# A top-32 attention feeding an MLP on one Trainium2 core: loads and stores on two DMA queues, weight preparation shared with GpSimd, new planner constants

## The chip, the cores and the metric

The kernel runs on one core of a Trainium2 chip. The metric is the device time of one execution in microseconds (us). Before the change it is 886.87 us, the median of three runs (886.37 to 887.69).

The engines are called here as the profile calls them: PE is TensorE (matmuls; PEld its weight loads), DVE is VectorE, ACT is ScalarE, POOL is GpSimd, SP is SyncE, which issues DMAs. Each engine works through its own list of instructions strictly in order.

## The reference

```python
# q, k, v: (4 batches, 8 heads, 576, 64) float32
scores = q @ k.T / sqrt(64)
kth    = 32nd largest of each row
attn   = softmax(where(scores >= kth, scores, -1e9))
x      = (attn @ v), heads side by side        # (2304, 512)
h      = x @ w_in                              # w_in (512, 2048)
g      = h * tanh(softplus(h))
return g @ w_out                               # w_out (2048, 512)
```

The two weight matrices arrive as 64-bit floats; everything else is float32.

## The kernel before, in words

The kernel holds three kinds of work, which one planner interleaves.

**Attention.** The unit of work (`unit`) is a tile of 128 query rows of a pair of heads; it has two "slots", one for each head (a last half tile of 64 rows has one slot), 144 slots in all. For a slot PE makes the scores (L604), ACT evicts them to SBUF as S (L621), DVE takes the eight largest of each of eight chunks of 72 columns (L636, eight per slot) and from these the first 24 of the row (L646, L650). Then all scores above the 24th are counted and masked, either by ACT with a Sign (L665) or by DVE (L669), POOL multiplies the mask with S (L673), a small instruction on DVE writes nine sentinels behind the row (L676), and DVE finds the 32nd largest from the rest (L679). ACT takes the exponential (L722) and DVE masks and sums it (L724). PE transposes the result (L769), ACT evicts it, PE multiplies with V (L805). K of a pair of heads is loaded by five DMAs (`dk`, L493 to L498), V by three (`dvl`, L526 to L530), a tile of Q by one (L571), all on SP.

**The weights.** `piece` takes 32 blocks of 128 x 512 numbers, 16 of `w_in` and 16 of `w_out`. Each block comes by one DMA of 512 KB on SP (L403), as pairs of 32-bit words. It is put together from the two words: a shift of the low word by 29 bits on DVE (L409), the high word scaled by ACT into PSUM (L414), and both joined by DVE (L424). The sign is taken in one of two ways: where `share(SGN, i)` is true, by a Sign on ACT (L418) and a product on POOL (L429); otherwise by one more DVE instruction (L420). All but the first six blocks of `w_out` are then split in two for the matmul's reduced format: ACT casts the high part (L440), and the low part is made either by PE and ACT (L446, L447, L450, where `share(PLO, i)` is true) or by a subtraction on POOL (L453).

**The MLP.** Nine groups of 256 tokens, each of 16 column blocks: PE multiplies with `w_in` (L906), ACT and POOL make the activation, PE multiplies with `w_out` (L975, L979). `flush` evicts a group's output (L998) and stores it (L1019, all on SP; the last group has eight stores).

**The order.** Nothing is ordered by hand. Every step is handed to `Plan.op` with an engine, an assumed duration, its dependencies, the buffers that it takes and frees, and a priority; `Plan.schedule` plays them through a model of the chip and writes the instructions out in the order that this gives. A step may name other engines in `also` (the helper `either` names POOL first, then DVE and sometimes ACT); the planner takes the one with the earliest assumed end, to which it adds an amount from `BIAS` for any but the first. The constants `MLP0`, `MLPS`, `LAG`, `OFF` and `WPO` set the priorities: of MLP groups against attention, of kinds of steps within a unit, and of `w_out` blocks. `PLO` and `SGN` are shares. For an SP step `cols` is the time that issuing takes and the duration that of the transfer:

```python
if o.eng == "sp":
    avail["sp"] = s + o.cols
    moved = max(s + o.cols + 0.65, moved) + o.dur
    o.end = moved + 0.9
```

After the plan, `rows_missed` checks on the chip that the first pass was exact, and a branch (L1071) skips a slow second pass.

Of the kernel before, what the change touches and what calls it, by code (L numbers as in the profile page):

```python
# [10 lines left out]
F32R = mybir.dt.float32r  # L11
I32 = mybir.dt.int32
AF = mybir.ActivationFunctionType
ALU = mybir.AluOpType
# [5 lines left out]
KHI = float(2.0 ** 27)  # L20
TOPK = 32
NCH = 8
PAD = 9
# [8 lines left out]
XR = 512  # L32
MLP0 = 59.16014052214167
MLPS = 1.1073074438698398
LAG = (-25.995810819941177, -17.66529125005204, -14.559786015886564, -11.242347655389478, -8.814713112832253, -7.76696476612947, -3.1712703340899724, -0.9827647919513685, -5.242546123881124)
OFF = (-9.344957211177771, 2.0041542064057873, -0.6528013842420144, 1.3086536928118269, 0.41279236860293267, 1.0938802916676011, -1.5617639856277443, 2.6926860599010802, -28.16820150226302, -2.1162741319410996, 2.930197754188401, -1.6831534370444627, 9.183328578610238)
WPO = 4.861214464413224
CSH = [(19, 0.8667247802625605), (999, 0.3323003066774938)]
MSH = [(11, 0.9149166775649588), (999, 0.13298644690001551)]
WPR = (19.149617763081373, 0.047652472774268644)  # L40
DELTA = 0
ALSO = True
N2 = 6
LOCK = True
TAB = 1.4
BIAS = [(54.23725795086648, 10.898476612244764), (712.3479862116446, 0.9005748864757063), (1000000000.0, 0.7950689159040172)]
PLO = [(11, 1.0), (999, 0.21870871979825823)]
SGN = 0.5127532531018606
PH = {3: ([0, 1], [2], [3, 4])}

SLACK = {'pe': 0.2487527268649277, 'dve': 0.0, 'act': 0.0, 'pool': 0.3}
TICK = 3.413
# [3 lines left out]
class Held(float):  # L58
    pass


# [13 lines left out]
class Plan:  # L75
# [22 lines left out]
    def schedule(self):  # L98
# [34 lines left out]
        while ndone < len(self.ops):  # L133
# [52 lines left out]
            if o.eng == "sp":  # L186
                avail["sp"] = s + o.cols
                moved = max(s + o.cols + 0.65, moved) + o.dur
                o.end = moved + 0.9
            else:  # L190
                o.end = avail[o.eng] = s + dur
                if o.eng == "pool" or isinstance(o.dur, Held):
                    port[o.eng] = o.end
# [23 lines left out]
def acts(n, bias=0, acc=0):  # L217
    return act(n, bias, acc) + 0.04
# [10 lines left out]
def dve2(n):  # L229
    return Held((0.5208 * n + 72) / 1000)  # L230
# [6 lines left out]
def pool1(n):  # L237
    return (1.03 * n + 110) / 1000
# [7 lines left out]
def attn_moe_kernel(  # L246
# [98 lines left out]
    def build(fast, weights):  # L345
# [22 lines left out]
        def share(part, n):  # L368
# [3 lines left out]
            return int((n + 1) * part) > int(n * part)  # L372

        xw = [[None] * (NT // 64) for _ in range(KC)]
        xread = [[[] for _ in range(NT // 64)] for _ in range(KC)]
# [4 lines left out]
        if weights:  # L380
# [7 lines left out]
            def piece(i, src, hi, lo, a, ready, pool):  # L388
# [12 lines left out]
                if wide:  # L401
                    val = lambda t=F32, e=0: word(e, t).rearrange("p (a b) -> p a b", a=a)
                    d = P.op("sp", 1.46, lambda: nc.sync.dma_start(  # L403
                        out=stage().bitcast(I32).rearrange("p (a b) -> p a b", a=a), in_=src),
# [75 lines left out]
            release("STG", [("HB", x) for x in range(Z["HB"] - 6, Z["HB"] - 2)])  # L480


        def pair_keys(b, p, ts, pr):
# [7 lines left out]
            def dk():  # L491
                kn_, rest = g_("KN", kn_key), k[b, 2 * p:2 * p + 2, T * 128:S, :].rearrange("h p d -> p h d")
                nc.sync.dma_start(out=kn_[:, 0:T, 1, :], in_=kap(1))  # L493
                nc.sync.dma_start(out=kn_[64:128, 0:T, 0, :], in_=kap(0)[0:64])
                nc.sync.dma_start(out=kn_[0:64, 1:T + 1, 0, :], in_=kap(0)[64:128])
                edge = kn_[0:64].rearrange("p t h d -> p (t h d)")
                for h, c_ in ((0, 0), (1, T * 2 * D + D)):
                    nc.sync.dma_start(out=edge[:, c_:c_ + D], in_=rest[:, h, :])  # L498

            kn_key = key + ("n",)  # L500
            d1 = [P.op("sp", 1.63, dk, alloc=[("KN", kn_key)], prio=pr - 3 + OFF[0], cols=2.9)]
# [23 lines left out]
            def dvl():  # L525
                nc.sync.dma_start(out=g_("V", key + ("v",)),  # L526
                                  in_=v[b, 2 * p:2 * p + 2, 0:T * 128, :].rearrange("h (p t) d -> p h t d", t=T))
                for h in range(2):
                    hp = slice(64 - 64 * h, 128 - 64 * h)
                    nc.sync.dma_start(out=vl[P.slot[key + ("v",)]][hp, h, :], in_=v[b, 2 * p + h, T * 128:S, :])  # L530

            dv = [P.op("sp", 0.9, dvl, alloc=[("V", key + ("v",))], prio=pr + OFF[2], cols=1.78)]
            return key, [v1, v2], dv

        slot_no = [0]
        shared = {}
        ends = dict(ot=[], rz=[], on=[])

        def either(tp, td, fn, deps, ta=None, fa=None, **kw):

            also = [("dve", td, lambda: fn(nc.vector))]
            if ta:
                also.append(("act", ta, fa))
            return P.op("pool", tp, lambda: fn(nc.gpsimd), deps, also=also if ALSO else (), **kw)

        def unit(b, p, t, pkey, kready, vready, last, pr, final):
# [25 lines left out]

            dq = [P.op("sp", 0.36, dql, alloc=[("QN", qn)], prio=pr - 3 + OFF[0], cols=0.5)]
            wq = key + ("wq",)
# [52 lines left out]
            if fast:  # L627
# [29 lines left out]
                for n in range(nt):  # L657
# [10 lines left out]
                    else:  # L668
# [193 lines left out]
        def group(g):  # L862
# [28 lines left out]
            for q_ in range(NQ):  # L891
                hk, hbk = ("h", g, q_), ("hb", g, q_)
                for e in range(2):
# [3 lines left out]
                    def m1(f=f, hk=hk, e=e):  # L897
# [10 lines left out]
                    mlp["m1"] = P.op("pe", 1.46, m1, cols=3072, deps=sp + wi_ready[f] + [mlp["m1"]],  # L908
                                     alloc=[("H", hk), ("HB", hbk)] if e == 0 else (),
# [38 lines left out]
        def second(u, g, q_, hbk, deps, pr):  # L948
# [14 lines left out]
            for e in range(2):  # L963
# [7 lines left out]
                def m2(f=f, e=e, glk=glk):  # L971
                    for t in range(GT // 128):
# [9 lines left out]
                mlp["oprev"] = P.op("pe", 1.72 if plain else 1.42, m2, cols=3072,  # L982
                                    deps=[o, mlp["oprev"]] + wo_ready[f], alloc=[("O", ok)] if f == 0 else (),
# [6 lines left out]
        def flush(g, pr):  # L990
# [3 lines left out]
            for t in range(GT // 128):  # L994
                for e in range(2):
# [15 lines left out]

                    def dma(segs=segs, eh=eh, obk=obk):
                        for o_, s, b, tt, r in segs:
                            if tt == T:
                                dst = out[b * S + T * 128 + r:b * S + T * 128 + r + s, :]
                            else:
                                dst = out[b * S:b * S + T * 128, :].rearrange(
                                    "(p t) n -> t p n", t=T)[tt, r:r + s, :]
                            nc.sync.dma_start(out=dst[:, eh], in_=g_("OB", obk)[o_:o_ + s, :])  # L1019

                    P.op("sp", 0.36, dma, [evs[-1]], free=[("OB", obk)], prio=pr, cols=0.6 * len(segs))
            evs[-1].deps += evs[:-1]
# [82 lines left out]
```

## Time and profile before

| what | value |
|---|---|
| median of three runs | 886.87 us (886.37 to 887.69) |
| profiled execution: its own time | 884.94 us |
| profiled execution: span from first to last instruction | 883.0 us |
| busy PE / DVE / ACT / POOL | 821.9 / 679.5 / 672.4 / 545.8 us |
| mean granted TensorE clock | 0.968 |

The profile is one execution. A row of a group of instructions gives the line of the kernel, engine, operation, output and inputs, shapes and count, then the busy time and the mean of one instruction, then the idle time of the engine just before them and what ended it. A table by stretches of time gives the busy time of each engine in each stretch. The chain is followed back from the last instruction, at each step to what released it; what is not on it ran beside it. "SPq" rows are DMA issues by SP; a transfer itself lands later.

### The profile page before, as it was taken

What the parts mean: (1) busy time and instruction counts of PE and PEld (TensorE: products, weight loads), DVE (VectorE), ACT (ScalarE), POOL (GpSimd) and SP (SyncE); (2) the same over time, 40 slices, a digit from 0 to 9 for tenths busy, and PEclk for the clock granted to TensorE, in tenths of its full rate; (3) what the DMA queues carried; (4) which work ended last, traced back from release to release, by engine and by line L of the source; (5) the groups of instructions that cost most, each with busy time, mean ns of one, the idle gap of its engine ahead of it and who ended that gap; (6) DMA issues with size and microseconds to landing.
All of it is one profiled execution on the core that took longest, in us unless ns stands there. A gap on an engine that the chain in (4) does not pass through costs nothing.

```text
span 883.0 us, 18617 instructions
## 1 busy us (share of the span) xinstructions
PE 821.9 (93%) x5755; PEld 607.1 (69%) x5755; DVE 679.5 (77%) x3331; ACT 672.4 (76%) x1422; POOL 545.8 (62%) x800
## 2 busy tenths in 40 slices
PE   6787796799899999999999999999999999999995
PEld 2454484476777577867786687767776778697963
DVE  5899899999789969977998979989987797311200
ACT  5989686988788887879779689778798668745640
POOL 2756654777775975469757676786655744623432
PEclk9889697899999999999999999999999999999998
DMA  6433233333112001201221111212121111000011
GB/s 160 116 108 110 71 104 106 108 102 95 35 33 60 22 22 36 58 18 34 50 54 28 33 25 27 52 32 50 35 59 36 43 29 29 15 21 4 1 25 29
DMA packets 87661, 45.81 MB, mean 52 GB/s; under 512 B 64768, under 2 KB 85504, under 8 KB 87552
## 3 DMA queue, kind: packets, MB, share of 16 engines
q1 hardware_dynamic: 87552, 44.53, 19.1%
q8 instruction: 48, 0.79, 0.4%
q14 instruction: 61, 0.50, 0.2%
HBM read 39.78 MB, written 4.72 MB: 50 GB/s over the span
## 4 chain that ended last, share of the span: by engine, by line
PE 55%; DVE 25%; ACT 9%; POOL 4%; issue 3%; DMA 2%; SPq 1%; POOLq 0%; ACTq 0%; DVEq 0%
PE psH L906 13%; PE psO L979 11%; PE psO L975 8%; DVE C L636 6%; PE psW L604 6%; PE psW L805 6%; PE psW L769 5%; DVE Y L724 4%; DVE M L679 3%; PE psW L906 3%; DVE C L650 2%; DVE M L646 2%; DVE Y L669 2%; POOL Y L673 2%; ACT Y L722 1%
## 5 line engine op out<-in xcount | busy, mean ns | idle before, releaser
L673 POOL TENSOR_TENSOR Y<-Y,S 128x576 f32<-128x576 f32 x139 | 196.5, 1427 | 41.4 <-ACT Y L665 17.2
L636 DVE MAX8 C<-S 128x8 f32<-128x72 f32 x1152 | 177.7, 220 | 15.9 <-ACT S L621 15.8
L906 PE MATMUL psH<-xh,wih 128*128 128x256 f32 x512 | 154.0, 301 | 0.1
L906 PE MATMUL psH<-xl,wih 128*128 128x256 f32 x512 | 143.8, 281 | 0.6 <-POOL xl L877 0.6
L906 PE MATMUL psH<-xh,wil 128*128 128x256 f32 x512 | 143.5, 280 | 0.0
L724 DVE SCALAR_TENSOR_TENSOR Y<-S,M,Y 128x576 f32<-128x576 f32 x121 | 113.2, 953 | 21.0 <-ACT Y L722 20.9
L621 ACT COPY S<-psW 128x288 f32<-128x288 f32 x288 | 105.5, 409 | 23.7 <-PE psW L604 21.9
L722 ACT ACTIVATE Y<-S,SM 128x576 f32<-128x576 f32 x121 | 92.4, 779 | 35.0 <-DVE M L679 34.1
L604 PE MATMUL psW<-KS,QS 64*128 64x288 f32 x512 | 108.5, 475 | 7.4 <-DVE mb L424 3.8
L679 DVE MAX8 M<-Y 128x8 f32<-128x585 f32 x144 | 109.2, 758 | 6.0 <-POOL Y L673 5.0
L769 PE MATMUL psW<-ident,Y 128*128 128x128 f32 (+1 forms) x640 | 87.2, 273 | 18.0 <-ACT S L621 8.1
L906 PEld LDWEIGHTS psH<-xh,wih 128*128 128x128 f32 x512 | 97.3, 190 | 8.8 <-issue 5.8
L769 PEld LDWEIGHTS psW<-ident,Y 128*128 128x128 f32 (+1 forms) x640 | 65.0, 141 | 50.1 <-issue 15.0
L906 PEld LDWEIGHTS psH<-xl,wih 128*128 128x128 f32 x512 | 97.0, 189 | 2.2 <-POOL xl L877 0.9
L975 PE MATMUL psO<-wof,mb 128*128 128x512 f32 x208 | 97.2, 601 | 0.1
L906 PEld LDWEIGHTS psH<-xh,wil 128*128 128x128 f32 x512 | 96.8, 189 | 0.0
L775 ACT COPY WT<-psW 128x512 f32<-128x512 f32 (+1 forms) x159 | 82.8, 547 | 11.4 <-PE psW L769 10.7
L805 PE MATMUL psW<-WT,V 128*64 128x128 f32 (+1 forms) x1280 | 86.2, 280 | 2.5 <-ACT WX L791 2.4
L805 PEld LDWEIGHTS psW<-WT,V 128*64 128x64 f32 x1280 | 67.7, 144 | 30.0 <-issue 9.5
L739 POOL TENSOR_SCALAR RB<-SM 128x64 f32<-128x64 f32 (+1 forms) x125 | 32.8, 280 | 81.1 <-DVE SM L731 40.7
L646 DVE MAX8 M<-C 128x8 f32<-128x64 f32 x432 | 81.2, 215 | 1.0
L979 PE MATMUL psO<-woh,GH 128*128 128x512 f32 x180 | 77.3, 430 | 0.0
(142 smaller groups left out, 1852.1 us busy)
## 6 DMA issues: line engine op xcount, KB each, us to landing
mb<-in_moe_w_in_dram SPq DMA_DIRECT2D x16, 512.0 KB, 3.9
mb<-in_moe_w_out_dram SPq DMA_DIRECT2D x16, 512.0 KB, 3.7
V<-in_v_dram SPq DMA_DIRECT2D x31, 256.0 KB, 2.8
QN<-in_q_dram SPq DMA_DIRECT2D x64, 64.0 KB, 2.0
KN<-in_k_dram SPq DMA_DIRECT2D x31, 128.0 KB, 2.7
KN<-in_k_dram SPq DMA_DIRECT2D x62, 64.0 KB, 2.6
out_dram<-OB SPq DMA_DIRECT2D x15, 128.0 KB, 1.9
out_dram<-OB SPq DMA_DIRECT2D x24, 64.0 KB, 2.2
```

The source lines that it names most:

```text
L604: nc.tensor.matmul(psW[P.slot[wks[n]]][:, 0:HS], g_(qpool, qs)[hp, :], KSt()[hp, rng], start=True, stop=True)
L621: return lambda: eng(St(n)[:, rng], psW[P.slot[w]][:, 0:HS])
L636: nc.vector.max(Ct(n)[:, j, :], St(n)[:, j * CW:(j + 1) * CW])
L673: y = either(pool2(S), held(S), lambda eng, n=n: eng.tensor_tensor(Yt(n), Yt(n), St(n), op=ALU.mult), [c], prio=pr + 0.5 + OFF[5])
L679: ym.append(P.op("dve", dve(S + PAD), lambda n=n: nc.vector.max(M8()[:, n, 3, :], Yw(n)), [y, x], prio=pr + 0.6 + OFF[6]))
L722: e = P.op("act", acts(S, 1), lambda n=n: nc.scalar.activation(Yt(n), St(n), AF.Exp, scale=scale, bias=SM()[:, 0, n:n + 1]), [nm, ym[n]], ...
L724: mk.append(P.op("dve", held(S, 60), lambda n=n: nc.vector.scalar_tensor_tensor(Yt(n), St(n), th(n), Yt(n), op0=ALU.is_ge, op1=ALU.mult, a ...
L769: nc.tensor.transpose(psW[P.slot[wk]][:, t_ * w:(t_ + 1) * w], Yt(n)[hp, c_:c_ + 128], ident[hp, hp])
L805: nc.tensor.matmul(psX[64 * h:64 * h + 64, 0:n_], lw, rhs, start=t_ == 0, stop=t_ == T)
L906: nc.tensor.matmul(w, a, b_, start=n == 0, stop=n == len(mm) - 1)
L975: nc.tensor.matmul(psO[t], hb_()[:, e, ts_], wof[:, f, :], start=f == 0, stop=f == NF - 1)
L979: nc.tensor.matmul(psO[t], c[:, ts_], y[:, f - N2, :], start=f == 0 and n == 0, stop=f == NF - 1 and n == 2)
```

## The change

- At the start, the first pair's K is loaded by two DMAs on SP and three on ACT's queue, and its V by three on ACT's queue. At the end, the four stores of the left output halves of the last group are issued by ACT, the other four by SP. `Sent` is the planner's class for a DMA issued by ACT.
- The shift of the low word is now a POOL step (a product and a sum that round to the same integer), with the DVE shift as the alternative. The cast of the high part is a POOL step, with DVE and ACT as alternatives. The sentinel instruction of a slot (L676) is a POOL step with DVE as the alternative.
- `SGN` falls from 0.513 to 0.368: 11 blocks instead of 16 take their sign by ACT and POOL. `PLO`: 13 instead of 14 blocks make their low part on PE, and the very first is now among the others.
- The planner's model of DMA times changes, and so do the priorities (groups 1 to 3 and 6 of the MLP earlier, blocks of `w_out` earlier) and `BIAS`.

```diff
+THREE = 2.0 ** -29 * (1 - 2.0 ** -14)
+HALF = 0.5 - 2.0 ** -12
-LAG = (-25.99, -17.67, -14.56, -11.24, -8.81, -7.77, -3.17, -0.98, -5.24)
+LAG = (-25.99, -26.47, -19.14, -18.85, -7.79, -8.80, -12.37, -1.67, -7.59)
-WPO = 4.861214464413224
+WPO = -0.6274142379880567
-BIAS = [(54.2, 10.9), (712.3, 0.9006), (1e9, 0.795)]
+BIAS = [(48.9, 12.9), (724.1, 0.9006), (1e9, 0.293)]
-PLO = [(11, 1.0), (999, 0.21870871979825823)]
-SGN = 0.5127532531018606
+PLO = [(16, 0.7434170351780047), (999, 0.21870871979825823)]
+SGN = 0.3679529210622342
...
+class Sent(float):
+    LAND = 2.1
...
-                moved = max(s + o.cols + 0.65, moved) + o.dur
-                o.end = moved + 0.9
+                moved = max(s + 1.2 * o.dur, moved) + o.dur
+                o.end = max(moved, s + o.cols) + 1.25
...
-                    o = P.op("dve", dve2(PN), lambda: nc.vector.tensor_scalar(
-                        word(0, I32), word(0, I32), 29, None, op0=ALU.logical_shift_right), [d], prio=pr)
+                    o = P.op("pool", pool1(PN) + 0.05, lambda: nc.gpsimd.tensor_scalar(
+                        word(0, I32), word(0, U32), THREE, -HALF, op0=ALU.mult, op1=ALU.add), [d], prio=pr,
+                        also=[("dve", dve2(PN), lambda: nc.vector.tensor_scalar(
+                            word(0, I32), word(0, I32), 29, None, op0=ALU.logical_shift_right))])
...
-                o = P.op("act", acts(PN), lambda: nc.scalar.copy(hi, val()), [o], prio=pr)
+                o = either(pool1(PN), dve2(PN), lambda eng: eng.tensor_scalar(
+                    hi, val(), 1.0, 0.0, op0=ALU.mult, op1=ALU.add), [o], acts(PN), lambda: nc.scalar.copy(hi, val()),
+                    prio=pr)
...
+                d1 = [P.op("sp", 0.55, lambda: dka(nc.sync), alloc=[("KN", kn_key)], prio=pr - 4 + OFF[0], cols=1.3),
+                      P.op("act", Sent(1.85), lambda: dkb(nc.scalar), prio=-1e9)]
...
+                dv = [P.op("act", Sent(1.7), lambda: dvl(nc.scalar), alloc=[("V", key + ("v",))], prio=-1e8)]
...
-                    x = P.op("dve", 0.07, lambda n=n: nc.vector.tensor_scalar(
+                    x = either(0.25, 0.07, lambda eng, n=n: eng.tensor_scalar(
...
+                    if g == NG - 1 and e == 0:
+                        P.op("act", Sent(0.6 * len(segs)), lambda dma=dma: dma(nc.scalar), [evs[-1]],
+                             free=[("OB", obk)], prio=pr + 1e3)
```

The constants are shown rounded in `LAG` and `BIAS`; `MLP0`, `MLPS` and `OFF` change too.

## Rows read from the trace of the kernel before

**Rows 1.** The page: busy time, share of the span, instructions of each engine.

```profile
PE 821.9 (93%) x5755; PEld 607.1 (69%) x5755; DVE 679.5 (77%) x3331; ACT 672.4 (76%) x1422; POOL 545.8 (62%) x800
```

**Rows 2.** Stretches: length, busy PE, PEld, DVE, ACT, POOL, clock, DMA share, GB/s.

```profile
0.00:25.00 25.00, 16.19 (x45) 7.96 (x45) 14.25 (x81) 14.26 (x32) 7.38 (x16) 1.00 0.61 163
...
225.00:725.00 500.00, 494.94 (x3693) 372.17 (x3694) 438.94 (x2251) 405.13 (x878) 344.26 (x508) 1.00 0.15 37
725.00:872.00 147.00, 146.44 (x936) 117.37 (x934) 37.97 (x119) 83.84 (x132) 63.19 (x85) 1.00 0.06 16
...
25.00:225.00 200.00, 164.25 (x1086) 109.58 (x1085) 188.22 (x882) 168.50 (x381) 130.96 (x192) 0.89 0.36 101
```

**Rows 3.** The chain of waits from 25 to 225 us, its shares by line.

```profile
by line: DVE C L636 10.5%; issue 7.8%; DVE Y L724 7.1%; POOL Y L673 5.9%; DVE M L679 5.6%; DMA mb<-in_moe_w_out_dram 4.7%; DVE C L650 4.4%; DVE M L646 4.3%; DVE mb L409 3.4%; ACT Y L665 3.2%; ACT psW L414 2.8%; ACT WT L775 2.7%; ACT Y L722 
```

**Rows 4.** The timeline of the first 12 us: start, duration, engine and line.

```profile
0.74 1.28 ACT L511 ACT_TABLE_LOAD   x1 [0.74 <-PEq L1089]
0.74 0.70 SPq L493 DMA_DIRECT2D KN<-in_k_dram  x1
...
2.80 1.25 SPq L498 DMA_DIRECT2D KN<-in_k_dram  x2
...
5.09 1.08 PE L506 MATMUL psW<-ident,KN 128*128 128x128 f32 x4 [5.09 <-DMA KN<-in_k_dram]
...
6.21 0.70 ACT L511 COPY KS<-psW 128x512 f32<-128x512 f32 x2 [4.20 <-PE psW L506]
6.40 1.69 SPq L403 DMA_DIRECT2D mb<-in_moe_w_in_dram  x3
...
10.57 0.43 DVE L409 TENSOR_SCALAR mb<-mb 128x512 int32<-128x512 int32 x1 [8.59 <-DMA mb<-in_moe_w_in_dram]
10.63 0.65 ACT L414 ACTIVATE psW<-mb 128x512 f32<-128x512 f32 x1 [3.45 <-DMA mb<-in_moe_w_in_dram]
11.21 0.69 ACT L621 COPY S<-psW 128x288 f32<-128x288 f32 x2
```

**Rows 5.** Groups by line and shape: count, busy us, mean ns, idle before.

```profile
L724 DVE SCALAR_TENSOR_TENSOR Y<-S,M,Y 128x576 f32<-128x576 f32 x121 | 113.2, 953 | 21.0 <-ACT Y L722 20.9
...
L429 POOL TENSOR_TENSOR mb<-mb 128x512 f32<-128x512 f32 x13 | 14.5, 1113 | 18.9 <-DVE mb L424 13.5 <-ACT S L621 2.3 <-ACT KS L511 1.4
...
L958 POOL TENSOR_SCALAR GH<-mb 128x512 fp32r<-128x512 f32 x25 | 16.6, 667 | 18.3 <-DVE mb L953 15.9 <-PE psO L979 2.2
L409 DVE TENSOR_SCALAR mb<-mb 128x512 int32<-128x512 int32 x32 | 16.6, 523 | 10.3 <-DMA mb<-in_moe_w_in_dram 9.9 <-DMA mb<-in_moe_w_out_dram 0.4
...
L676 DVE TENSOR_SCALAR Y<-ranks,SM 128x9 f32<-128x9 f32 x87 | 18.4, 211 | 0.6
...
L662 POOL TENSOR_SCALAR blog<-M 128x1 f32<-128x1 f32 x57 | 13.6, 242 | 23.2 <-DVE M L646 20.9
...
L418 ACT ACTIVATE mb<-mb 128x512 f32<-128x512 f32 x16 | 11.2, 699 | 0.1
L420 DVE SCALAR_TENSOR_TENSOR mb<-psW,mb 128x512 int32<-128x512 int32 x16 | 11.0, 687 | 0.7 <-ACT psW L414 0.3
L440 ACT CAST wih<-mb 128x512 fp32r<-128x512 f32 x16 | 11.0, 686 | 0.8 <-POOL mb L429 0.8
```

**Rows 6.** Single lines: ns of one, shortest/median/longest; L724 is that of 25 to 225 us.

```profile
L409 DVE TENSOR_SCALAR mb<-mb x32: 408/422/1506, 10.6 to 211.2; 128x512 int32<-128x512 int32 x32
...
L724 DVE SCALAR_TENSOR_TENSOR Y<-S,M,Y x29: 800/812/1753, 44.3 to 223.8; 128x576 f32<-128x576 f32 x29
```

**Rows 7.** The timeline from 871 us on: the last evictions and stores.

```profile
871.71 2.38 SPq L1019 DMA_DIRECT2D out_dram<-WT  x4
...
872.28 0.38 ACT L998 COPY WT<-psO 128x256 f32<-128x256 f32 x1
...
876.13 1.18 SPq L1019 DMA_DIRECT2D out_dram<-WT  x2
```

**Rows 8.** The closing branch on SP: ns of one, first and last start.

```profile
L1071 SPq COMPARE_BRANCH  x1: 50/50/50, 878.5 to 878.5; - x1
```

More of the change, by code (lines that the diff above doesn't have):

```diff
@@ L12 @@
 I32 = mybir.dt.int32
+U32 = mybir.dt.uint32
 AF = mybir.ActivationFunctionType
@@ L32 @@
 XR = 512
[L33 to L36, printed above, removed]
-WPO = 4.861214464413224
-CSH = [(19, 0.8667247802625605), (999, 0.3323003066774938)]
-MSH = [(11, 0.9149166775649588), (999, 0.13298644690001551)]
+MLP0 = 58.83975636082121
+MLPS = 1.121860262315038
+LAG = (-25.995810819941177, -26.474079155792758, -19.13806320546605, -18.854128398230255, -7.786063767408372, -8.799346239468274, -12.371711128172647, -1.6692882578445132, -7.591562462708602)
+OFF = (-16.98515120479643, 2.328093500794843, -3.96944656014681, 3.035426527996102, 0.4828418529158596, 0.7164642923464081, -1.649352757422735, 0.6592529327519733, -28.765739384772523, -3.5228328815861154, 6.763792071250068, -2.9083787972029063, 9.183328578610238)
+WPO = -0.6274142379880567
+CSH = [(18, 0.8667247802625605), (999, 0.3323003066774938)]
+MSH = [(11, 0.919392917195224), (999, 0.13298644690001551)]
 WPR = (19.149617763081373, 0.047652472774268644)
@@ L187, in schedule @@
                 avail["sp"] = s + o.cols
-                moved = max(s + o.cols + 0.65, moved) + o.dur
-                o.end = moved + 0.9
+                moved = max(s + 1.2 * o.dur, moved) + o.dur
+                o.end = max(moved, s + o.cols) + 1.25
             else:
                 o.end = avail[o.eng] = s + dur
+                if isinstance(o.dur, Sent):
+                    o.end += Sent.LAND
                 if o.eng == "pool" or isinstance(o.dur, Held):
@@ L372, in share, with either @@
             return int((n + 1) * part) > int(n * part)
+        def either(tp, td, fn, deps, ta=None, fa=None, **kw):
+            also = [("dve", td, lambda: fn(nc.vector))]
+            if ta:
+                also.append(("act", ta, fa))
+            return P.op("pool", tp, lambda: fn(nc.gpsimd), deps, also=also if ALSO else (), **kw)
         xw = [[None] * (NT // 64) for _ in range(KC)]
@@ L480, in build @@
             release("STG", [("HB", x) for x in range(Z["HB"] - 6, Z["HB"] - 2)])
+        shared = {}
         def pair_keys(b, p, ts, pr):
@@ L488, in kap, with dka, dkb, dk @@
                 return k[b, 2 * p + h, 0:T * 128, :].rearrange("(p t) d -> p t d", t=T)
-            def dk():
+            def dka(eng):
+                kn_ = g_("KN", kn_key)
+                eng.dma_start(out=kn_[:, 0:T, 1, :], in_=kap(1))
+                eng.dma_start(out=kn_[64:128, 0:T, 0, :], in_=kap(0)[0:64])
+            def dkb(eng):
                 kn_, rest = g_("KN", kn_key), k[b, 2 * p:2 * p + 2, T * 128:S, :].rearrange("h p d -> p h d")
-                nc.sync.dma_start(out=kn_[:, 0:T, 1, :], in_=kap(1))
-                nc.sync.dma_start(out=kn_[64:128, 0:T, 0, :], in_=kap(0)[0:64])
-                nc.sync.dma_start(out=kn_[0:64, 1:T + 1, 0, :], in_=kap(0)[64:128])
+                eng.dma_start(out=kn_[0:64, 1:T + 1, 0, :], in_=kap(0)[64:128])
                 edge = kn_[0:64].rearrange("p t h d -> p (t h d)")
                 for h, c_ in ((0, 0), (1, T * 2 * D + D)):
-                    nc.sync.dma_start(out=edge[:, c_:c_ + D], in_=rest[:, h, :])
+                    eng.dma_start(out=edge[:, c_:c_ + D], in_=rest[:, h, :])
+            def dk():
+                dka(nc.sync)
+                dkb(nc.sync)
             kn_key = key + ("n",)
-            d1 = [P.op("sp", 1.63, dk, alloc=[("KN", kn_key)], prio=pr - 3 + OFF[0], cols=2.9)]
+            begin = not shared
+            if begin:
+                shared["begun"] = True
+                d1 = [P.op("sp", 0.55, lambda: dka(nc.sync), alloc=[("KN", kn_key)], prio=pr - 4 + OFF[0], cols=1.3),
+                      P.op("act", Sent(1.85), lambda: dkb(nc.scalar), prio=-1e9)]
+            else:
+                d1 = [P.op("sp", 0.9, dk, alloc=[("KN", kn_key)], prio=pr - 3 + OFF[0], cols=3.1)]
             def tr():
@@ L523, in pair_keys, with dvl @@
             v2 = P.op("act", act(64), ev(512, 64, w2), [t2], free=[("W", w2)], prio=pr - 2 + OFF[1])
-            def dvl():
-                nc.sync.dma_start(out=g_("V", key + ("v",)),
+            def dvl(eng):
+                eng.dma_start(out=g_("V", key + ("v",)),
                                   in_=v[b, 2 * p:2 * p + 2, 0:T * 128, :].rearrange("h (p t) d -> p h t d", t=T))
@@ L529, in dvl @@
                     hp = slice(64 - 64 * h, 128 - 64 * h)
-                    nc.sync.dma_start(out=vl[P.slot[key + ("v",)]][hp, h, :], in_=v[b, 2 * p + h, T * 128:S, :])
-            dv = [P.op("sp", 0.9, dvl, alloc=[("V", key + ("v",))], prio=pr + OFF[2], cols=1.78)]
+                    eng.dma_start(out=vl[P.slot[key + ("v",)]][hp, h, :], in_=v[b, 2 * p + h, T * 128:S, :])
+            if begin:
+                dv = [P.op("act", Sent(1.7), lambda: dvl(nc.scalar), alloc=[("V", key + ("v",))], prio=-1e8)]
+            else:
+                dv = [P.op("sp", 0.9, lambda: dvl(nc.sync), alloc=[("V", key + ("v",))], prio=pr + OFF[2], cols=1.75)]
             return key, [v1, v2], dv
         slot_no = [0]
-        shared = {}
         ends = dict(ot=[], rz=[], on=[])
[L539 to L544, printed above, removed]
         def unit(b, p, t, pkey, kready, vready, last, pr, final):
@@ L571, in dql @@
                 nc.sync.dma_start(out=g_("QN", qn)[0:64 if isl else 128], in_=src)
-            dq = [P.op("sp", 0.36, dql, alloc=[("QN", qn)], prio=pr - 3 + OFF[0], cols=0.5)]
+            dq = [P.op("sp", 0.2, dql, alloc=[("QN", qn)], prio=pr - 3 + OFF[0], cols=0.5)]
             wq = key + ("wq",)
@@ L1010, in flush, with dma @@
                         o_ += s
-                    def dma(segs=segs, eh=eh, obk=obk):
+                    def dma(eng, segs=segs, eh=eh, obk=obk):
                         for o_, s, b, tt, r in segs:
@@ L1018, in dma @@
                                     "(p t) n -> t p n", t=T)[tt, r:r + s, :]
-                            nc.sync.dma_start(out=dst[:, eh], in_=g_("OB", obk)[o_:o_ + s, :])
-                    P.op("sp", 0.36, dma, [evs[-1]], free=[("OB", obk)], prio=pr, cols=0.6 * len(segs))
+                            eng.dma_start(out=dst[:, eh], in_=g_("OB", obk)[o_:o_ + s, :])
+                    if g == NG - 1 and e == 0:
+                        P.op("act", Sent(0.6 * len(segs)), lambda dma=dma: dma(nc.scalar), [evs[-1]],
+                             free=[("OB", obk)], prio=pr + 1e3)
+                    else:
+                        P.op("sp", 0.36, lambda dma=dma: dma(nc.sync), [evs[-1]], free=[("OB", obk)], prio=pr,
+                             cols=0.6 * len(segs))
             evs[-1].deps += evs[:-1]
```

10 lines of the change are left out of this document (5 added, 5 removed).

## The prediction

> **What bounds the kernel now.** I first read the busy shares of the engines [rows 1]: PE is busy for 93% of the span, so at first sight nothing but PE counts. The table by stretches corrects this [rows 2]. From 225 to 725 us PE is busy for 494.9 of 500 us and from 725 to 872 us for 146.4 of 147: there PE alone sets the pace, and a step taken off another engine gains nothing. From 25 to 225 us it is different. PE is busy for 164.3 of 200 us, so 35.7 us are idle, while DVE is busy for 188.2, ACT for 168.5 and POOL for 131.0. This is the stage in which the weights are put together beside the attention. The granted clock there is 0.89, which is a mix of the two levels: PE, with gaps in its work, is for part of the time at 1.2 GHz, and at 2.4 GHz once it is full. Since PE's total work hardly changes and nothing but PE counts after 225 us, a gain can come from three places alone: the start, the idle PE time in this stage, and what follows PE's last matmul.
>
> The chain of waits for that stage says what paces it [rows 3]. Of the lines that it lists, DVE's (L636, L724, L679, L650, L646, L409) sum to 35.3% of the stage, and L409, the shift that the change takes off DVE, holds 3.4% or 6.8 us by itself. ACT's lines L665, L414 and L775 sum to 8.7%, POOL's one line (L673) is 5.9%.
>
> In the timeline of the start [rows 4], SP issues K, Q and V one after another, and so the first weight block only at 6.40 us. ACT waits for it 3.45 us with L414 at the head of its list, until 10.63, and the first eviction of scores (L621) stands behind that, at 11.21 us. DVE's first useful instruction starts at 10.57 us after 8.59 us idle. At the end [rows 7, 8], the last eviction is over at 872.66 us, but SP issues eight stores from 871.71 to 877.31 and branches at 878.5.
>
> **The change part by part.**
>
> *The start.* SP's nine issues from 0.74 to 6.40 us take 0.63 each. With three of K and three of V gone to ACT, three stand before the first weights: 0.74 + 3 x 0.63 = 2.6 us, so 3.8 us earlier. On ACT six issues stand ahead of L511. No row shows a DMA issued by ACT; I price it as SP's, 0.63, and then the table load of 1.28 ends at 0.74 + 6 x 0.63 + 1.28 = 5.8 us, still ahead of 6.21, when ACT starts now. If the table load comes first, the last part of K is issued 1.3 us later, at 3.9 instead of 4.05 us, and K gains almost nothing. The ends are therefore 0.4 us (ACT's start) and 3.8 us (the weights, on which ACT's list stood). I take 2.5, nearer to the weights, since the wait that ended last was theirs, but not all of it, since all these transfers now run together on DMA engines that were busy for 0.61 of these 25 us [rows 2].
>
> *DVE's relief in the stage.* The 32 shifts take 16.6 us [rows 5]. Five blocks more take their sign by L420: 5 x 0.687 = 3.4 us back. The stage holds 29 of the 121 L724 [rows 5, 6], so about 34 of the 144 sentinels; at 0.211 that is 7.2 us, but these short DVE instructions overlap their neighbours, so I count half, 3.6. Relief: 16.6 - 3.4 + 3.6 = 16.8 us. Its worth lies between the chain's share of DVE, 0.35, and 1, if DVE were the only pacer: 5.9 to 16.8 us. As DVE is busy for 94% of the stage but the chain often leaves it, I take 0.45: **-7.6 us**.
>
> *ACT's relief.* I let POOL take 16 of the 26 casts: 16 x 0.686 = 11.0 us, and five Signs of 0.699 less are 3.5. With ACT's 8.7% of the chain: **-1.3 us**.
>
> *POOL's load.* The shift on POOL is not in the trace, nor any POOL step with whole numbers. The nearest rows are L958, as many elements from one input, 0.667 us, and L429, the same interleaved words but two inputs, 1.113 us [rows 5]. I take 0.667, since it has one input like the shift: 32 x 0.667 = 21.3 us. The casts cost 16 x 0.667 = 10.7, the sentinels 34 x 0.242 = 8.2 (the price of L662), five products fewer 5.6 less, and one more subtraction adds about a product's 1.1. The sum is 36 us: POOL goes from 131 to 167 of 200 us. That still leaves it below DVE (188 - 17 = 171). By its share of the chain, 36 x 0.059: **+2.1 us**.
>
> *POOL against DVE.* The DVE instructions that work beside POOL are stretched now and then: L409 takes 0.422 us in the median and 1.506 at worst, L724 0.812 and 1.753 [rows 6], and all L724 average 0.953 [rows 5], 0.14 over that median. With POOL a quarter fuller I add a quarter to this, 0.035, and for a stage in which other DVE steps suffer too, **+1.1 us** (29 x 0.035 = 1.0). The Trainium skill (GPSIMD Engine Reference, Specifications) says that POOL shares its SBUF interfaces with VectorE and contends with DVE instructions that run in a two-port mode or have two SBUF inputs. That speaks against this change, since every step moved to POOL could hold an L724. So far the trace agrees only in a few cases: the median L724 is 12 ns above the shortest. What it would make of the time is the fourth rival below.
>
> *PE's part.* One block fewer makes its low part on PE. In a stage with 35.7 us of idle PE I count that as nothing; if the cover is gone, it is a small gain.
>
> *The stores.* Eight issues take 5.6 us [rows 7], 0.70 each. ACT has nothing behind its four but the branch, and its evictions end at 872.66, so the two queues end at about 874.5 to 875.4. I take **-2.8 us**, four issues. The bounds are nothing, if two issuers only take turns, and 3.1, if SP starts as early as now and does four.
>
> *Priorities and the DMA model.* They only change the order. After 225 us PE never waits long, so a new order there is covered by PE's own queue; before, earlier MLP groups could fill idle PE or hold ACT and POOL up. I count nothing, with 4 us on either side.
>
> The sum is -2.5 - 7.6 - 1.3 + 2.1 + 1.1 - 2.8 = **-11.0 us**. The profiled execution took 884.94 us, 1.93 below the median of the runs. 884.94 - 11.0 = 873.9, and as runs go 875.9: I predict 876.
>
> **The rivals.**
>
> *The ends alone (881.6 us).* POOL, fuller, paces the stage as DVE did, or the planner leaves most shifts and casts where they were (DVE and ACT remain as alternatives), and only start and end gain: 886.9 - 2.5 - 2.8. For it: the four engines are near each other (171, 154, 167, 164 of 200 by the sums above), so the next one soon ends the gain. Against it: the chain has L409 itself on it for 6.8 us, and these go.
>
> *DVE as the only pacer (864.8 us).* Relief counts in full: 886.9 - 16.8 - 5.3. For it: DVE's 94%. Against it: the chain, which is on DVE's listed lines for only a third.
>
> *POOL becomes the bound (894 us).* If the shift costs more than L429, say 1.5 us, and POOL takes all 26 casts, POOL has 131 + 48 + 17 + 8 - 4 = 200 us of work in a stage where the fullest engine now manages 188 in 200; 200/188 x 200 = 212, so +12 us, with -5.3 at the ends +7. It decides from a POOL load of about 188 us, which a shift of 1.1 us would give: 131 + 35.6 + 17.3 + 8.2 - 4.5 = 188. For it: no row shows such a shift on POOL, and POOL steps behind a late weight block wait in order, L673 with them, and DVE's L679 behind that. Against it: one-input steps on POOL are cheap [rows 5].
>
> *POOL holds DVE (895 us).* Each of the stage's 29 L724 is stretched once by one of the added POOL steps, by 0.667 us: 19 us more on the engine that the chain is on most, so 886.9 - 11.0 + 19.3. For it: the longest L724 and L409, about 1 us over their medians [rows 6]. Against it: POOL was busy for 65% of the stage already, and the median L724 hardly felt it. The page named above states such contention.
>
> *No change to speak of (887 us).* Losses of order eat what the ends gain.
>
> **How the numbers follow.** A measurement of this kernel can tell about 0.2% from no change, 1.8 us. I give the forecast 0.51 (868 to 881), the ends alone 0.20 (880 to 885), DVE as the only pacer 0.12 (861 to 868), POOL as the bound 0.10 (889 to 900), POOL holding DVE 0.03, no change 0.04. Faster is thus 0.82 (0.83 less a little of the ends case that comes out within the bound), same 0.05, slower 0.13. The range reaches from 866, which takes in the upper part of the large gain, to 886, past the ends alone; what lies outside is the two slow cases, part of no change and the far end of the large gain.
>
> **What would show it.** Right: the first weight DMA issued near 2.6 us and DVE at work by about 8; between 25 and 225 us DVE's busy share lower, POOL's near 83%, PE's idle time some 6 us less, so PE full from about 217 us on; PE's last matmul near 864; SP's branch about 3 us after the last eviction instead of 5.8. Shift rows on POOL near 0.67 us. Wrong: shifts of 1.1 us or more; idle time of DVE's L679 behind L673; PE as idle before 225 us as now; or the closing branch as late after PE as before.

## The result, and the profile after

The changed kernel takes 872.37 us (median of four runs, 872.00 to 873.14) where the kernel before took 887.28 beside it: a ratio of 0.9834, 95% interval 0.9817 to 0.9851. That is 14.9 us less, clear of the noise, inside the range and 3.6 us below the predicted 876. The profiled execution took 873.14 us, its span is 871.3.

The page and the table by stretches, in the same columns as [rows 1, 2]:

```profile
PE 811.7 (93%) x5752; PEld 603.1 (69%) x5752; DVE 680.6 (78%) x3265; ACT 657.9 (76%) x1398; POOL 568.0 (65%) x885
```
```profile
25.00:225.00 200.00, 163.48 (x1069) 110.02 (x1071) 177.35 (x820) 162.79 (x361) 171.56 (x267) 0.88 0.36 100
225.00:725.00 500.00, 497.60 (x3792) 377.50 (x3790) 433.80 (x2196) 408.95 (x890) 370.14 (x576) 1.00 0.15 38
```

Between 25 and 225 us DVE's busy time falls from 188.2 to 177.4 us and POOL's rises from 131.0 to 171.6. PE's does not rise. From 225 to 725 us PE is a little fuller than before (497.6 us of 500, 494.9 before), and it is done sooner: its last matmul of the MLP ends at 871.98 us before and at 861.56 now, 10.4 us earlier. Since the idle time of PE up to 225 us is 44.6 us before (225 less the 180.4 busy of that stretch) and 47.6 now, the gain does not lie in idle time before 225 us but in how much work PE still had ahead of it then. Its busy time over the whole run falls by 10.2 us, 821.9 to 811.7. The group that falls most is the matmuls that make the low parts of the weights, in the first 225 us (L446, L447 in the kernel before; L469, L470 in the changed kernel):

```profile
L446 PE MATMUL psW<-mb,ident 128*128 128x512 f32 x28 | 20.7, 826 | 2.0 <-POOL Y L673 0.8 <-ACT wil L450 0.7 <-ACT WT L775 0.2
L447 PE MATMUL psW<-wih,minus 128*128 128x512 f32 x12 | 12.2, 1018 | 0.0
L447 PE MATMUL psW<-woh,minus 128*128 128x512 f32 x2 | 2.1, 1064 | 0.0
...
L469 PE MATMUL psW<-mb,ident 128*128 128x512 f32 x26 | 15.4, 674 | 3.8 <-POOL blog L696 1.0 <-ACT WT L809 1.0 <-POOL wih L461 1.0
L470 PE MATMUL psW<-wih,minus 128*128 128x512 f32 x11 | 9.6, 872 | 0.0
L470 PE MATMUL psW<-woh,minus 128*128 128x512 f32 x2 | 1.6, 818 | 0.0
```

They sum to 35.0 us before, for 14 blocks, and to 26.6 now, for 13. One block is about 2.5 of the 8.4 us; the rest is a lower mean (826 ns before, 674 now for the first group). L446 took 0.61 us at the shortest and 1.22 at the longest, a factor of two as between the two levels of the clock, and its median falls from 0.718 to 0.613 us (L469): I read this as fewer of them at the low level. Groups of matmuls overlap one another, so 8.4 us of a group are not 8.4 of the 10.2; what they are worth is answered by an experiment below.

The chain of waits from 25 to 225 us, as in [rows 3]:

```profile
by line: POOL Y L707 12.7%; issue 8.6%; DVE C L670 5.9%; POOL mb L428 4.4%; DVE M L713 4.2%; POOL Y L710 3.3%; POOL wol L476 3.2%; DVE Y L758 3.1%; POOL mb L987 2.6%; DVE mb L441 2.6%; DVE M L680 2.5%; DVE C L684 2.4%; DVE mb L445 2.4%; POO
```

It has gone over in part from DVE to POOL, whose listed lines now sum to 26.2%, while DVE's fall from 35.3% to 23.1%: L707 is the masked product (L673 before), 5.9% then and 12.7% now, and the shift (L428) and the sentinel (L710) stand on it as POOL steps. DVE now waits for POOL, as the list of waits up to 225 us shows (us in total, times, longest); the first line is of the kernel before, where L679 is what L713 is now:

```profile
DVE M L679 <- POOL Y L673: 1.7, 3, 0.6
...
DVE mb L441 <- POOL mb L428: 9.9, 6, 6.7
DVE M L713 <- POOL Y L707: 9.0, 11, 2.2
```

The wait for the product has grown from 1.7 to 9.0 us. Of L441's 9.9 us, 6.7 are the one wait for the first weight block, at the start. The prices of the new POOL steps, and of the DVE step that might have been held up by them, over the whole run as in [rows 5]:

```profile
L758 DVE SCALAR_TENSOR_TENSOR Y<-S,M,Y 128x576 f32<-128x576 f32 x121 | 111.6, 936 | 30.2 <-ACT Y L756 29.9
...
L428 POOL TENSOR_SCALAR mb<-mb 128x512 int32<-128x512 uint32 x32 | 23.0, 720 | 12.9 <-DMA mb<-in_moe_w_in_dram 9.0 <-DMA mb<-in_moe_w_out_dram 1.6
L710 POOL TENSOR_SCALAR Y<-ranks,SM 128x9 f32<-128x9 f32 x57 | 22.3, 392 | 26.2 <-DVE SM L764 12.7 <-DVE Y L703 11.0 <-DVE M L680 0.7
...
L710 POOL TENSOR_SCALAR Y<-sranks,SM 128x9 f32<-128x9 f32 x48 | 18.1, 377 | 13.3 <-ACT Y L699 10.4
```

The same DVE step in the stage alone, from 25 to 225 us, before and now:

```profile
L724 DVE SCALAR_TENSOR_TENSOR Y<-S,M,Y 128x576 f32<-128x576 f32 x29 | 25.8, 905 | 0.0
...
L758 DVE SCALAR_TENSOR_TENSOR Y<-S,M,Y 128x576 f32<-128x576 f32 x30 | 29.0, 976 | 3.0 <-ACT Y L756 2.9
```

Over the whole run its mean falls from 0.953 to 0.936 us, but in the stage it rises from 0.905 to 0.976: 11 of 30 took over 1 us, where 4 of 29 did before.

The start in the timeline, as in [rows 4]:

```profile
0.73 0.67 ACTq L523 DMA_DIRECT2D KN<-in_k_dram  x1
...
3.04 1.80 SPq L422 DMA_DIRECT2D mb<-in_moe_w_in_dram  x3
...
4.60 1.28 ACT L625 ACT_TABLE_LOAD   x1 [4.60 <-DMA KN<-in_k_dram]
...
7.99 0.62 ACT L435 ACTIVATE psW<-mb 128x512 f32<-128x512 f32 x1 [1.83 <-DMA mb<-in_moe_w_in_dram]
...
8.54 0.69 ACT L550 COPY KS<-psW 128x512 f32<-128x512 f32 x2
...
12.85 0.69 ACT L655 COPY S<-psW 128x288 f32<-128x288 f32 x2
```

The weights are taken up at 7.99 us instead of 10.63. But in ACT's list the waits for weight blocks (L435) stand ahead of the eviction of K (6.21 before, 8.54 now) and of the first scores (11.21 before, 12.85 now): attention starts later.

The end, as in [rows 7, 8]:

```profile
861.17 0.39 PE L1013 MATMUL psO<-woh,GL 128*128 128x512 f32 x1
...
861.31 1.16 ACTq L1053 DMA_DIRECT2D out_dram<-WT  x2
861.58 2.48 SPq L1053 DMA_DIRECT2D out_dram<-WT  x4
...
862.56 1.20 ACTq L1053 DMA_DIRECT2D out_dram<-OB  x2
```
```profile
L1110 SPq COMPARE_BRANCH  x1: 45/45/45, 865.2 to 865.2; - x1
```

SP branches 3.6 us after PE's last matmul instead of 6.5, so 2.9 us earlier; but the span ends 9.7 us after that matmul instead of 11.0, so only 1.3 of them reach the end in this execution.

### The profile page after: what moved, and what is told of

The parts are those of the page before. It is cut to its first block, busy times and chain, and to the rows that moved or that the text cites. A ratio compares the mean times of both kernels' runs of the same rounds, so it can differ in the third digit from the quotient of the medians.

```text
span 871.3 us, 18564 instructions
## 1 busy us (share of the span) xinstructions
PE 811.7 (93%) x5752; PEld 603.1 (69%) x5752; DVE 680.6 (78%) x3265; ACT 657.9 (76%) x1398; POOL 568.0 (65%) x885
## 4 chain that ended last, share of the span: by engine, by line
PE 71%; POOL 11%; DVE 9%; ACT 5%; issue 2%; DMA 2%; SPq 0%; DVEq 0%; POOLq 0%; ACTq 0%
PE psH L940 17%; PE psO L1013 14%; PE psO L1009 9%; PE psW L638 9%; PE psW L839 8%; PE psW L803 6%; POOL Y L707 3%; PE psW L940 3%; DVE C L670 2%; DVE Y L758 2%; DVE M L713 1%; PE psW L545 1%; PE psW L612 1%; POOL mb L428 1%; PE psW L817 1%
## 5 line engine op out<-in xcount | busy, mean ns | idle before, releaser
L707 POOL TENSOR_TENSOR Y<-Y,S 128x576 f32<-128x576 f32 x137 | 193.5, 1421 | 0.1
L670 DVE MAX8 C<-S 128x8 f32<-128x72 f32 x1152 | 175.7, 219 | 14.1 <-ACT S L655 13.5
L940 PE MATMUL psH<-xh,wih 128*128 128x256 f32 x512 | 151.3, 295 | 0.0
L758 DVE SCALAR_TENSOR_TENSOR Y<-S,M,Y 128x576 f32<-128x576 f32 x121 | 111.6, 936 | 30.2 <-ACT Y L756 29.9
L655 ACT COPY S<-psW 128x288 f32<-128x288 f32 x288 | 102.7, 407 | 35.8 <-PE psW L638 34.2
L713 DVE MAX8 M<-Y 128x8 f32<-128x585 f32 x144 | 109.4, 760 | 18.6 <-POOL Y L707 17.7
L638 PE MATMUL psW<-KS,QS 64*128 64x288 f32 x512 | 105.1, 477 | 10.1 <-DVE mb L445 3.8
L803 PEld LDWEIGHTS psW<-ident,Y 128*128 128x128 f32 (+1 forms) x640 | 67.4, 144 | 48.5 <-issue 12.3
L1009 PE MATMUL psO<-wof,mb 128*128 128x512 f32 x208 | 99.7, 609 | 0.8 <-POOL mb L987 0.8
L809 ACT COPY WT<-psW 128x512 f32<-128x512 f32 (+1 forms) x154 | 80.5, 549 | 7.3 <-PE psW L803 6.1
L703 DVE TENSOR_SCALAR_CACHE_REDUCE Y<-S,M 128x576 f32<-128x576 f32 x87 | 69.7, 804 | 5.5 <-PE psW L819 3.2
```

Of the source, the lines that this page charges most:

```text
L638: nc.tensor.matmul(psW[P.slot[wks[n]]][:, 0:HS], g_(qpool, qs)[hp, :], KSt()[hp, rng], start=True, stop=True)
L655: return lambda: eng(St(n)[:, rng], psW[P.slot[w]][:, 0:HS])
L670: nc.vector.max(Ct(n)[:, j, :], St(n)[:, j * CW:(j + 1) * CW])
L707: y = either(pool2(S), held(S), lambda eng, n=n: eng.tensor_tensor(Yt(n), Yt(n), St(n), op=ALU.mult), [c], prio=pr + 0.5 + OFF[5])
L713: ym.append(P.op("dve", dve(S + PAD), lambda n=n: nc.vector.max(M8()[:, n, 3, :], Yw(n)), [y, x], prio=pr + 0.6 + OFF[6]))
L758: mk.append(P.op("dve", held(S, 60), lambda n=n: nc.vector.scalar_tensor_tensor(Yt(n), St(n), th(n), Yt(n), op0=ALU.is_ge, op1=ALU.mult, a ...
```

## The experiments

Times of different runs are compared through their ratios to the kernel before, which ran beside each; 0.001 is 0.9 us. The intervals are 0.002 to 0.003 to each side, so a difference between two kernels is known to 2 to 4 us.

**Steps, or constants?** In the first pair, each kernel got the other's priorities and `BIAS` (and POOL's assumed wait).

```diff
# old_constants: the changed kernel
-MLP0, MLPS, LAG, OFF, WPO, BIAS, SLACK = (the changed kernel's)
+MLP0, MLPS, LAG, OFF, WPO, BIAS, SLACK = (those of before)
# new_constants_only: the kernel before, the other way round
```

> The changed kernel with the priorities and BIAS of before (MLP0, MLPS, LAG, OFF, WPO, BIAS and POOL's slack); queues, steps, shares and DMA model stay changed. Theory A, the moved steps and the two queues carry the gain as costed: about 876 us, 11 below before. Rival B, the gain lies in the order that the new constants give: 882 us or more, with only the two ends gained. Rival C, constants and steps fit only together: above 887.

> The kernel before with the new priorities and BIAS and nothing else. A: within 3 us of before, 884 to 890. B: 876 to 881. C: above 890, since these constants were set for a planner that may give POOL the shifts.

Measured: 903.4 us, ratio 1.0185 (1.0152 to 1.0218), and 899.0 us, 1.0137 (1.0103 to 1.0171). Rival C held in both: neither half alone gains anything, each loses 12 to 16 us. Theory A failed here: it costed the steps and counted the order as nothing.

**Does the order matter, or are those constants wrong for these steps?** The smallest possible change of the order, once in each kernel:

```diff
# changed_reshuffled; before_reshuffled likewise
-SLACK = {..., 'pool': 0.3014222492564422}
+SLACK = {..., 'pool': 0.3114222492564422}
```

> The changed kernel with one number of the planner altered by almost nothing: the wait that it assumes before a POOL step, 0.30 us, is 0.01 longer. Steps, engines and shares stay, the order comes out anew from early on. If the order of the recorded plan is itself worth much (as the run with the old constants, 903, suggests): 880 to 900. If any sensible order does, and the old constants were merely wrong for these steps: 870 to 876.

> The same 0.01 us added in the kernel before. If the order is worth much: 893 to 912, as far above 887 as the run with the new constants (899) or more. If any sensible order does: 884 to 890. With the run beside it, the difference between the two reshuffled kernels is what the moved steps give to an order that nobody chose: 10 to 15 by theory A, near 0 if the gain lies in the chosen order alone.

Measured: 897.2 us, 1.0130 (1.0103 to 1.0158), and 903.4 us, 1.0198 (1.0169 to 1.0226). A hundredth of a microsecond in one assumption costs the changed kernel 26 us and the kernel before 18. (The planner also chose engines a little differently: in the changed kernel reshuffled 19 casts run on POOL instead of 16, and 101 sentinels instead of 105.) The two differ by 6 us, less than theory A's 10 to 15. With the first pair there are two orders for each set of steps that nobody chose for it: 897.2 and 903.4 with the new steps, 899.0 and 903.4 with the old. The new steps are ahead in one pair and behind in the other, so among such orders these four kernels show no gain. Where part of the time goes is in the table by stretches of the changed kernel reshuffled:

```profile
225.00:475.00 250.00, 240.34 (x1796) 180.99 (x1796) 219.82 (x1110) 199.31 (x436) 181.61 (x281) 0.98 0.14 35
475.00:725.00 250.00, 245.92 (x1814) 184.71 (x1812) 198.52 (x979) 195.37 (x419) 175.65 (x274) 1.00 0.16 38
```

PE is idle there for 13.7 us, against 2.4 in the changed kernel's own order (225 to 725 us above) and 5.1 before [rows 2]. Its busy time over the run is longer too, 824.8 us against 811.7, for the same number of matmuls. So "after 225 us nothing but PE counts" is a property of the recorded orders, not of the kernel.

**What the steps are worth in a fixed order.** In these kernels the planner decides exactly as in the changed kernel, and only the engine that a step is issued on is put back; PE's list and SP's stay the same, row for row.

```diff
# shift_on_dve: planned as a POOL step, issued on DVE
-o = P.op("pool", pool1(PN) + 0.05, lambda: nc.gpsimd.tensor_scalar(word(0, I32), word(0, U32), THREE, -HALF, ...
+o = P.op("pool", pool1(PN) + 0.05, lambda: nc.vector.tensor_scalar(word(0, I32), word(0, I32), 29, None, ...
...
# sentinels_on_dve
-x = either(0.25, 0.07, lambda eng, n=n: eng.tensor_scalar(
+x = either(0.25, 0.07, lambda eng, n=n: nc.vector.tensor_scalar(
...
# casts_on_act: where the plan says POOL
+nc.scalar.copy(hi, val()) if eng is nc.gpsimd else eng.tensor_scalar(...
# shifts_and_sentinels_on_dve: the first two; three_steps_back: all three
```

> The changed kernel with the 32 shifts issued on DVE, at the places that the plan gives them, all else in the same order. Theory A, DVE paces the stage before 225 us and is relieved: 16.6 us more on DVE at 0.45, less what POOL gets back, so about 6 us slower, 878. Rival B, the engine of a step matters little while the order stays: within 3 us, 871 to 875. Rival D, DVE alone paces: 885 or more.

> The changed kernel with the 105 sentinel instructions that the plan puts on POOL (0.385 us each by its profile, where 0.24 was costed) issued on DVE at 0.21, same order. A: DVE gets back some 3.6 us before 225 us at 0.45, POOL loses more: 1 us slower, 873. Rival: DVE's L713 waits for POOL's L707 17.7 us in the changed kernel and 5.0 before, so POOL is the later of the two and this is faster: 869 to 871.

> The changed kernel with the 16 casts that the plan puts on POOL issued on ACT, same order. A: 11 us more on ACT at its 9% of the chain, POOL 11 us less: within 1 us, 871.4 to 873.4. Rival, ACT's list is what holds PE (its evictions): 2 us slower or more, above 874.4.

> Shifts and sentinels on DVE and casts on ACT at once, in the order of the changed kernel. A: the sum, 7 to 9 us slower, 879 to 882. Rival B (order): within 4 us, below 877. If more than the sum of the three single runs, the engines' loads add up to a new bound.

> The changed kernel with shifts and sentinels back on DVE, casts left on POOL, same order. Alone they cost 4.6 and 0.3 us, the casts 0.6, all three 12.0. If DVE alone becomes the pacer once it has both: 880 to 884, nearly all of the 12. If the excess comes from ACT's casts beside a full DVE: 876 to 878.

| issued back on | median us | ratio (interval) | against 0.9834, us |
|---|---|---|---|
| shifts on DVE | 876.96 | 0.9892 (0.9861 to 0.9923) | +5.1 |
| sentinels on DVE | 872.71 | 0.9836 (0.9809 to 0.9862) | +0.2 |
| casts on ACT | 872.99 | 0.9847 (0.9822 to 0.9871) | +1.2 |
| shifts and sentinels on DVE | 881.76 | 0.9952 (0.9930 to 0.9975) | +10.5 |
| all three | 884.38 | 0.9964 (0.9945 to 0.9983) | +11.5 |

The last column is the difference of the ratios times 887. So in the order that belongs to them, the moved steps are worth 11.5 us of the 14.9, give or take 2.3. All three back cost more than A's 7 to 9 and more than the sum of the single runs, the third outcome that the expectation names. The shifts came out between A's 6 and B's 3, too close to either to tell; sentinels and casts are each worth nothing that can be told by themselves. But shifts and sentinels together cost about twice their sum, as the expectation of the pair had it: once DVE has both, it paces again. Its stage, its chain, its page and its low parts, with the pair back on DVE:

```profile
25.00:225.00 200.00, 160.75 (x1011) 106.41 (x1011) 187.50 (x848) 157.04 (x348) 132.89 (x196) 0.86 0.34 98
```
```profile
by line: DVE C L670 15.6%; DVE Y L758 8.8%; DVE M L713 6.6%; DVE mb L428 6.2%; DVE mb L445 6.1%; DVE M L680 5.3%; issue 4.9%; DVE C L684 4.9%; DVE Y L703 4.9%; PE psW L803 4.9%; DVE mb L441 4.3%; PE psW L638 3.8%; PE psO L1009 3.5%; PE psH 
```
```profile
PE 818.4 (93%) x5752; PEld 606.0 (69%) x5752; DVE 706.9 (80%) x3402; ACT 658.0 (75%) x1398; POOL 506.3 (57%) x748
```
```profile
L469 PE MATMUL psW<-mb,ident 128*128 128x512 f32 x26 | 16.1, 703 | 2.4 <-POOL SM L745 0.8 <-DVE mb L445 0.7 <-issue 0.5
L470 PE MATMUL psW<-wih,minus 128*128 128x512 f32 x11 | 9.5, 860 | 0.0
L470 PE MATMUL psW<-woh,minus 128*128 128x512 f32 x2 | 1.5, 736 | 0.0
```

DVE is at 187.5 of 200 us, the load of before (188.2), the first place on the chain that is not DVE's is "issue" with 4.9%, and PE's last matmul ends at 872.63 us, 11.1 later than in the changed kernel with the same list of PE instructions. Of these 11.1 us only 4.4 are idle time of PE; 6.7 are busy time, since the same matmuls take 818.4 us instead of 811.7, with a granted clock of 0.86 instead of 0.88 in the stage. And the low parts take 27.1 us, nearly as little as in the changed kernel (26.6): their 8.4 us came with the new order and are not what the moved steps gain.

**The stores.**

```diff
# stores_one_queue
-if g == NG - 1 and e == 0:
+if False:
```

> The changed kernel with all eight last stores on SP; the order of everything else stays as it is. A, four issues of 0.70 us leave the path: 2.8 us slower than the changed kernel, 875.2. Rival, what follows SP's branch takes up part of it, as the profile of the changed kernel has only 1.3 us less behind PE's last matmul: 873.5 to 874.

Measured: 874.04 us, 0.9857 (0.9832 to 0.9882): 1.7 us by the medians, 2.0 by the ratios. The interval is as wide as the difference, so it lies between the rival's 1.3 and A's 2.8 and excludes neither. In the profiles the span ends 11.5 us after PE's last matmul, against 9.7 in the changed kernel. One thing more changed in the finished kernel than was expected: the last eviction of the output went from DVE to ACT.

**The start.**

```diff
# start_one_queue: K's rest and V on SP, same plan
-lambda: dkb(nc.scalar)    lambda: dvl(nc.scalar)
+lambda: dkb(nc.sync)      lambda: dvl(nc.sync)
# scores_before_weights: in the finished order, K's eviction is put ahead of the
# first L435, the first eviction of scores and DVE's first L670 ahead of the second,
# each with all that it depends on
```

> The changed kernel with the six first loads of K and V that ACT issues put on SP, at the places that the plan gives them; all other instructions in the same order on every engine. The first weight block is then issued three issues later, 1.9 us. A, the start is worth what the weights gain: 1.5 to 2.5 us slower than the changed kernel, 874 to 875. Rival, the first scores are evicted later in the changed kernel than before (12.85 against 11.21 us), so the start is lost again in ACT's order: within 0.8 us, 871.6 to 873.2.

> The changed kernel with one thing moved in its lists: ACT evicts the first K and the first scores before it waits for the first and second weight block, and DVE's first L670 follow, which in the changed kernel come at 8.54, 12.85 and 13.28 us. If the start lies on the path as I costed it: 1.5 to 4 us faster, 868 to 871. If the stage takes its time from elsewhere, so that the start is worth nothing either way: 871.5 to 873.5.

Measured: 872.89 us, 0.9843 (0.9815 to 0.9870), and 871.97 us, 0.9844 (0.9821 to 0.9867). The rival held both times: within 1 us. But the first kernel moved less than expected: its first weight block is issued at 4.66 us instead of 3.04 and taken up by ACT at 8.84 instead of 7.99, so only 0.85 us of the start were tested, and its first scores are evicted at 12.50 us, a little earlier than 12.85. The second kernel did what it was to do at first, and lost most of it again at once (its lines are numbered differently: L562 is L550, L669 is L655):

```profile
7.09 0.70 ACT L562 COPY KS<-psW 128x512 f32<-128x512 f32 x2 [0.59 <-PE psW L557]
...
9.09 0.70 ACT L669 COPY S<-psW 128x288 f32<-128x288 f32 x2 [0.50 <-PE psW L652]
...
13.94 0.70 ACT L669 COPY S<-psW 128x288 f32<-128x288 f32 x2 [0.64 <-PE psW L652]
```

The first scores are evicted at 9.09 instead of 12.85 us, the second pair at 13.94 instead of 15.07, behind two more waits for weights. It isn't a faster kernel than the changed one, as far as the intervals tell, and none of the other experiments is.

## Why the prediction was right, and where it was not

**The stage that decides.** That what happens before 225 us decides was right: PE's last matmul came 10.4 us earlier by way of that stage. The form was wrong. I looked for the gain in PE's idle time, 6 us less; it is 3 us more. So two of the signs that I had named for being wrong came: PE is as idle before 225 us as it was, and L713 waits for L707. What fell is PE's busy time, by 10.2 us, where the prediction says that "PE's total work hardly changes" and counts PE's part as nothing. The pair of steps put back shows why idle time was the wrong place to look: there PE loses more in longer matmuls (6.7 us) than in gaps (4.4).

**DVE's relief.** The mechanism held and the net was too small. The costed net of the stage was 7.6 + 1.3 - 2.1 - 1.1 = 5.7 us; in a fixed order the moved steps alone, without the five blocks whose sign goes the other way, are worth 11.5. For shifts and sentinels the terms of the sum are 20.2 us of relief at 0.45, so 9.1, less 1.7 for their load on POOL and 1.1 for POOL against DVE: 6.3 us, where the runs show 10.5. The weight of 0.45 need not be what was wrong: DVE's busy time over the run rises by 26.3 us when both go back (680.6 to 706.9), which makes 0.40 for each microsecond. The half price for the sentinels held as well: 105 of them back on DVE at 0.21 us raise its busy time by 10.9 us (691.5 against 680.6), 0.10 each. What the runs do not show is the cost that was set against the relief for POOL's load: POOL goes back from 171.6 to 132.9 us in the stage, and the kernel is only slower. Load alone does not price a step either: the shifts alone and the sentinels alone both bring DVE to about 184 of 200 us, and the one costs 5.1 us, the other 0.2. Why is not shown.

**ACT's relief.** 1.3 us costed, with the five Signs. The casts alone, put back on ACT, cost 1.2 us by the ratios and 0.6 by the medians, which is within the noise.

**POOL's load.** Costed 167 of 200 us, measured 171.6; the shift 0.667 costed, 0.720 measured; the sentinel 0.242 costed, 0.38 measured. POOL took a large part of DVE's place on the chain, as the first rival had it, but at a lower load than DVE's before, and DVE with 177.4 us is still the fuller of the two.

**POOL against DVE.** In the stage the mean of this step rises by 0.071 us, twice the 0.035 costed: 2.1 us over 30 instructions instead of 1.0. The rival built on it, with 19 us, failed. The contention that the Trainium skill states (GPSIMD Engine Reference, Specifications) agrees with single long instructions in this trace: of the 28 L758 over 1 us in the whole run, 26 start while a POOL instruction runs and end 0.60 to 0.62 us after that one has ended. But with POOL back at 132.9 us (shifts and sentinels on DVE) the mean is still 0.960 us, so the price does not simply follow POOL's load.

**The start.** 2.5 us costed; 0.5 (medians) to 0.8 (ratios) measured, for a test that moved the weights by 0.85 us only, so the term is neither confirmed nor refuted by it. Evicting the first scores 3.8 us earlier gained nothing that can be told. The weights did come earlier (3.04 us for 2.6 predicted, DVE at work at 8.71 for "about 8"). What "I take 2.5, nearer to the weights" left out is that the weights' wait was also put ahead of the scores in ACT's list, where the scores lose 1.6 us while the weights gain 2.6.

**The stores.** 2.8 us costed, 1.7 to 2.0 measured. Two issuers do work at once (ACT from 861.31 to 862.47, 0.58 us for one; SP from 861.58 to 864.06, 0.62), the branch came 2.9 us earlier as costed, and part of that was lost in the closing sequence behind it. What holds that sequence up was not tried.

**Priorities.** "They only change the order" and "I count nothing, with 4 us on either side" were the gravest misjudgement, though the sum survived it: an order that does not fit costs 12 to 26 us here, more than the whole gain. It survived by luck: both recorded kernels seem to have orders that fit their steps, so that the difference of the two is close to what the steps and the two queues are worth in a fixed order, 11.5 + 2.0 + 0.8 = 14.3 of the measured 14.9 us. Each of the three is known to 2 to 3 us only, and that they add up was not tried. The forecast missed the gain by 3.6 us because a net that was too small in the stage stands beside ends that were counted too large or cannot be confirmed.

What stays open: why an order with the same steps leaves PE idle after 225 us. The runs show that it does (13.7 against 2.4 us), not which step of the order begins it. The smaller parts of the change were not put back one by one: the signs (`SGN`), the block that no longer makes its low part on PE (`PLO`), the planner's DMA model and some of its assumed durations, and the shares `CSH` and `MSH`, which change slightly as well. Nor were the steps moved in the order of the kernel before.

## What to carry to other kernels

When an engine at 94% paces a stage, ask how far the engine that bounds the rest of the kernel has come at the end of that stage: what it loses there can lie in its busy time as well as in its gaps. Put moved steps back together as well as singly: here two cost 5.1 and 0.2 us alone and 10.5 together. And read a step's price in the stage that decides, not over the whole run: here one mean rose in the stage while it fell over the run. In a kernel whose order a planner makes, test a step by putting it back in the finished order, not by planning anew: a change of 0.01 us in one assumption moved this kernel by more than the change under study. And before counting on an earlier first transfer, read which other work the list of the waiting engine has behind that wait.

## What the runs showed of the hardware that was not expected

A shift of whole numbers by a product and a sum with rounding runs on POOL at nearly the price of a floating-point step of the same size: 0.720 us in the mean and 0.662 in the median for 128x512 from unsigned to signed integers, where the one-input floating-point step before took 0.667 [rows 5] and 0.619. Small steps are dear there: nine elements in each partition take 0.38 us on POOL and 0.21 on DVE. And a long DVE step of two inputs (L758) is one that waited out a POOL step: its end comes 0.60 to 0.62 us after that step's end, 26 times of 28.
